# A fused attention and feed-forward kernel on one core: its 2074 steps emitted in another order

## The chip, the core and the metric

The kernel runs on one core of a Trainium2 chip. A core has five engines with a queue of instructions each: TensorE (PE, matmuls, with its weight loads shown as PEld), VectorE (DVE), ScalarE (ACT), GpSimd (POOL) and SyncE (SP). Here SP issues all transfers. Each queue is worked through in the order in which the program emitted its instructions; between queues only semaphores order the work. The metric is device time in microseconds, the median of repeated runs.

## The reference

Inputs q, k and v are (8, 8, 576, 64): batch, head, token, head width. Two attentions are added and the sum goes through a feed-forward block:

```python
# pooled: means over 4 tokens, softmax attention over 144, repeated 4 times
out_up = repeat(softmax(scale * q_d @ k_d.T) @ v_d, 4)
# local: a band of |i - j| < 4
out_local = softmax(where(abs(i - j) < 4, scale * q @ k.T, -1e9)) @ v
x = (out_up + out_local)            # as (4608 tokens, 512)
h = x @ w_in                        # 512 -> 1024
solu = h * softmax(h)
ln = (solu - mean) / sqrt(var + 1e-6) * g_ln
out = ln @ w_out                    # 1024 -> 512
```

The weights come as 64-bit floats. The products of the feed-forward block are done in three parts (high x high, high x low, low x high) to keep their precision.

## The kernel before, in words

The work is cut into steps, and a step is what a Python generator does between two `yield`s: mostly one engine's instructions. A list `plan` holds all 2074 of them in a fixed numbering (lines 948 to 959), and `ORDER` (lines 26 to 125) is a list of these numbers. Lines 961 to 964 turn the scheduler off and call the steps in `ORDER`'s sequence, so that `ORDER` is the program order, and its projection on each engine is that engine's queue. Buffers rotate in this sequence too: a tile with a tag of one buffer can be taken only when the last reader of the tile before is done.

The steps, by the names that the text uses:

- **Batch b, prepare** (`load_q_k`, then `pair_steps` for each of four pairs of heads): q and k are loaded and transposed, in batches 0 to 2 on TensorE (`qp`, `kp`, line 463, with ScalarE's copy at 469), from batch 3 on VectorE (lines 390 and 394). VectorE then sums groups of four tokens (`qds`, `kds`, line 348). The q and k tiles have tags of one buffer.
- **Batch b, values**: four loads `vs` (line 260) with GpSimd sums (lines 415 and 418).
- **Batch b, local, five blocks u** (`by_tensor`): load `lv` (line 249); `sc` 32 small matmuls (591); on VectorE mask and maximum (603, 608); on GpSimd a subtraction (610); on ScalarE exp (612); on VectorE sum and reciprocal (615, 619); on GpSimd a product (621); on TensorE `plt`, four transposes (631); ScalarE's copy (634); `xp`, 32 matmuls (641); and the result goes into x (480 on ScalarE, 482 on VectorE).
- **Batch b, pooled, four pairs** (`Pooled`): `sd` (667), maximum (674), exp (682 to 686), reciprocal (689), GpSimd's product (691), `pdt` (702), two copies (709 on ScalarE, 714 on VectorE from batch 2 on), `po` (723), and VectorE's addition into x (482; in batch 0 it is ScalarE's copy that begins x).
- **Weights, 16 pieces** (`Weights`): a load (297), ScalarE's absolute value (305), four VectorE steps (307, 311, 316, 320) that make a 32-bit float out of the halves of a 64-bit one, a rounding to the high part on ScalarE (341; pieces 8 to 15 are multiplied by g_ln first, 339), and the low part on GpSimd (343). Pieces 0 to 7 are w_in, 8 to 15 w_out.
- **Tile i of 128 tokens, in** (`xhl`, `ffn_in`): ScalarE's cast xh (890), GpSimd's rest xl (893), `h` in two halves of 12 large matmuls (741), maximum on VectorE (749), exp on ScalarE (753), product on VectorE (756), small GpSimd steps (761, 765), ScalarE's shift by the mean (778), the write of the tile to DRAM as `u` (784), a reciprocal (787), the sum of squares (793) and the small steps to the scale s (790 to 800). `ffn_back` reads `u` back as `v`, rearranged, in four transfers (816).
- **Tile i, out** (`ffn_ut`, `ffn_out`): two VectorE transposes of 32x32 blocks (837), ScalarE's cast uh (843) and the rest ul (845, GpSimd; VectorE from tile 29 on) for each half, `o` in two halves of 12 large matmuls (859), ScalarE's scaling to osb (866), and the store (868). Tile 35 is transposed by TensorE instead (`ut`, 833).

PSUM has eight banks and is divided thus: `ps_a` two tiles of two banks (`sc`, `sd`, `pdt`, `xp`, `qp`, `kp` in turn), `ps_t` one bank (`plt` and `po`; in batches 0 and 1 every other one goes to `ps_o`), `ps_h` two banks (`h`), `ps_o` one bank (`o`).

In the old list the part from batch 2 on is regular: one `h` and one `o` of 24 large matmuls in turn, with one to four small blocks between them.

Of the kernel before, what the change touches and what calls it, by code (L numbers as in the profile page):

```python
# [128 lines left out]
def pooled_local_attention_then_solu_ffn(  # L129
# [142 lines left out]


    class Weights:
        def begin(self):
            stage = att.tile([P, NPR, S], F32, tag="x", name="stage", bufs=2)
            self.stage = stage.rearrange("p a s -> p (a s)")
            self.g = cpool.tile([P, NFC], F32, name="g_sb")
# [718 lines left out]
```

## Time and profile before

| | |
|---|---|
| median of 3 runs | 630.46 us (628.94 to 631.41) |
| span of the profiled execution | 627.6 us (its own time isn't given beside it) |
| TensorE busy | 577.7 us, 92% |
| VectorE, ScalarE, GpSimd busy | 393.4, 370.4, 380.8 us |
| chain that ended last | TensorE 62%, VectorE 11%, SP's queue 8%, transfers 7% |
| bytes moved by the transfers | 94.31 MB, 150 GB/s on average |

The span runs from the first to the last instruction of one execution. Lines of the profile name the source line, engine, operation, output and inputs, shapes, and a count; busy time is followed by the mean in ns; "[0.61 <-DVE x L482]" is idle time ahead of an instruction and what ended it. In the rows of busy time by stretches the columns are the stretch, its length, then busy us (and instructions) of PE, PEld, DVE, ACT and POOL, the granted clock of TensorE (1.00 is full), the busy share of the DMA engines, and GB/s.

### The profile page before, as it was taken

The numbers are of one execution on the slowest core, as the hardware profiler recorded it, in microseconds if no ns is written. First come the engines' busy times: TensorE is split into PE (matmuls) and PEld (weight loads), VectorE is DVE, ScalarE is ACT, GpSimd is POOL, SyncE is SP. The second block draws the span as 40 slices with busy tenths as digits, with TensorE's granted clock in tenths as the row PEclk, the third lists the DMA queues.
The fourth block names the chain that finished last, engine by engine and source line by source line (L and its number), as shares of the span: only waits on it lengthen the run. The fifth ranks groups of instructions, "written<-read, shape, count | busy, mean of one in ns | idle before, by whom it ended". The sixth has DMA issues, their size and how long they took to land.

```text
span 627.6 us, 14806 instructions
## 1 busy us (share of the span) xinstructions
PE 577.7 (92%) x5624; PEld 451.6 (72%) x5624; DVE 393.4 (63%) x684; ACT 370.4 (59%) x808; POOL 380.8 (61%) x552
## 2 busy tenths in 40 slices
PE   1677789989999998999999899999999999999997
PEld 1456557777777776777777677777777777788875
DVE  6988869775745683678536783679356534453541
ACT  3667586865753565547745575556855675454451
POOL 2486668969734894469636893589646974242210
PEclk9985879969999998999999899999999999999999
DMA  9997994668668878664678477824542232224320
GB/s 233 263 195 210 191 218 119 175 131 174 157 173 177 179 177 180 165 170 139 158 160 196 120 172 154 192 95 138 159 142 71 70 118 85 85 84 154 98 101 34
DMA packets 210055, 94.31 MB, mean 150 GB/s; under 512 B 171712, under 2 KB 198848, under 8 KB 209984
## 3 DMA queue, kind: packets, MB, share of 16 engines
q1 hardware_dynamic: 209984, 93.37, 60.1%
q8 instruction: 44, 0.72, 0.5%
q14 instruction: 27, 0.22, 0.1%
HBM read 65.54 MB, written 27.79 MB: 149 GB/s over the span
## 4 chain that ended last, share of the span: by engine, by line
PE 62%; DVE 11%; SPq 8%; DMA 7%; ACT 5%; issue 4%; POOL 3%; DVEq 0%; POOLq 0%; ACTq 0%
PE o L859 25%; PE h L741 23%; SPq L230 4%; DMA v<-u 3%; PE xp L641 3%; PE plt L631 3%; PE po L723 2%; DMA u<-e 2%; PE sd L667 2%; SPq L816 2%; PE sc L591 2%; DVE w L316 1%; DVE nmx L749 1%; DVE v L837 1%; PE pdt L702 1%
## 5 line engine op out<-in xcount | busy, mean ns | idle before, releaser
L859 PE MATMUL o<-wo_h,uh 128*128 128x512 f32 x288 | 118.8, 412 | 4.3 <-ACT uh L843 3.6
L741 PE MATMUL h<-wi_h,xh 128*128 128x512 f32 x288 | 119.9, 416 | 3.0 <-ACT xh L890 2.7
L741 PE MATMUL h<-wi_h,xl 128*128 128x512 f32 x288 | 116.7, 405 | 0.5 <-POOL xl L893 0.4
L741 PE MATMUL h<-wi_l,xh 128*128 128x512 f32 x288 | 116.3, 404 | 0.0
L859 PE MATMUL o<-wo_l,uh 128*128 128x512 f32 x288 | 115.6, 401 | 0.0
L845 POOL TENSOR_TENSOR ul<-v,uh 128x512 fp32r<-128x512 f32 x58 | 74.5, 1293 | 25.3 <-ACT uh L843 20.4
L749 DVE TENSOR_REDUCE nmx<-h 128x1 f32<-128x1024 f32 x36 | 43.6, 1212 | 59.8 <-PE h L741 59.8
L859 PE MATMUL o<-wo_h,ul 128*128 128x512 f32 x288 | 79.4, 397 | 0.2 <-POOL ul L845 0.2
L859 PEld LDWEIGHTS o<-wo_h,uh 128*128 128x128 f32 x288 | 55.1, 191 | 18.5 <-ACT uh L843 4.0
L741 PEld LDWEIGHTS h<-wi_h,xh 128*128 128x128 f32 x288 | 55.7, 193 | 16.7 <-ACT xh L890 3.1
L741 PEld LDWEIGHTS h<-wi_h,xl 128*128 128x128 f32 x288 | 55.4, 192 | 15.4 <-POOL xl L893 2.0
L859 PEld LDWEIGHTS o<-wo_h,ul 128*128 128x128 f32 x288 | 54.6, 190 | 14.1 <-POOL ul L845 0.7
L741 PEld LDWEIGHTS h<-wi_l,xh 128*128 128x128 f32 x288 | 55.9, 194 | 12.1
L837 DVE STREAM_TRANSPOSE v<-v 128x512 f32<-128x512 f32 x70 | 46.6, 691 | 27.9 <-DMA v<-u 27.6
L859 PEld LDWEIGHTS o<-wo_l,uh 128*128 128x128 f32 x288 | 55.2, 192 | 12.0
L843 ACT ACTIVATE uh<-v 128x512 fp32r<-128x512 f32 x70 | 43.5, 625 | 27.6 <-DVE v L837 18.9
L753 ACT ACTIVATE e<-h,nmx 128x1024 f32<-128x1024 f32 x36 | 40.1, 1113 | 32.4 <-DVE nmx L749 32.0
L893 POOL TENSOR_TENSOR xl<-x,xh 128x512 fp32r<-128x512 f32 (+1 forms) x40 | 47.3, 1185 | 19.4 <-ACT xh L890 19.3
L610 POOL TENSOR_TENSOR pl<-pl,mxl 128x512 f32<-128x512 f32 x40 | 42.4, 1068 | 22.6 <-DVE mxl L608 22.5
L793 ACT ACTIVATE e<-e 128x1024 f32<-128x1024 f32 x35 | 36.9, 1054 | 31.3 <-DMA u<-e 31.0
L778 ACT ACTIVATE e<-e,nmu 128x1024 f32<-128x1024 f32 x35 | 40.2, 1147 | 18.1 <-POOL nmu L761 18.0
L621 POOL TENSOR_TENSOR pl<-pl,rsl 128x512 f32<-128x512 f32 x40 | 42.0, 1056 | 13.8 <-DVE rsl L619 10.0
(92 smaller groups left out, 1084.9 us busy)
## 6 DMA issues: line engine op xcount, KB each, us to landing
u<-e SPq DMA_DIRECT2D x35, 512.0 KB
v<-u SPq DMA_DIRECT2D x140, 128.0 KB
vw<-in_v_dram SPq DMA_DIRECT2D x160, 64.0 KB
vs<-in_v_dram SPq DMA_DIRECT2D x32, 288.0 KB
out_dram<-osb SPq DMA_DIRECT2D x36, 256.0 KB
qm<-in_q_dram SPq DMA_DIRECT2D x80, 72.0 KB
km<-in_k_dram SPq DMA_DIRECT2D x80, 72.0 KB
w<-in_moe_w_out_dram SPq DMA_DIRECT2D x8, 512.0 KB
```

The source lines that it names most:

```text
L610: nc.gpsimd.tensor_tensor(out=pl, in0=pl, in1=max_bc, op=ALU.subtract)
L621: nc.gpsimd.tensor_tensor(out=pl, in0=pl, in1=rs.unsqueeze(3).broadcast_to([P, NPR, 2, W]), op=ALU.mult)
L741: nc.tensor.matmul(hps[:, n, :], src[:, cc, :], wt[:, cc, n * 512:(n + 1) * 512], start=(cc == 0 and src is xh and wt is wi_h), stop=(cc = ...
L749: nc.vector.tensor_reduce(out=nmx, in_=hf, op=ALU.max, axis=AX.X, negate=True)
L753: nc.scalar.activation(e, hf, AF.Exp, bias=nmx, scale=1.0, accum_out=se)
L778: nc.scalar.activation(e, e, AF.Identity, bias=nmu, scale=1.0)
L793: nc.scalar.activation(e0, e, AF.Square, accum_out=m2)
L837: nc.vector.transpose(vg, vg)
L843: nc.scalar.activation(uh, tp, AF.Copy)
L845: (nc.vector if v is None or i in LATE else nc.gpsimd).tensor_tensor(out=ul, in0=tp, in1=uh.bitcast(F32), op=ALU.subtract)
L859: nc.tensor.matmul(o, src[:, j, :], wt[:, 4 * g + j, :], start=(g == 0 and j == 0 and src is uh and wt is wo_h), stop=(g == 1 and j == 3 a ...
L893: nc.gpsimd.tensor_tensor(out=l, in0=src, in1=h.bitcast(F32), op=ALU.subtract)
```

## The change

The list `ORDER` is another permutation of the same steps. Three things in the code go with it, so that steps of a batch can come in any sequence: a batch's buffers are made when first asked for (`__getattr__`) and no longer by the step of pair 0; the weights' staging buffer is made by the first piece that uses it; and the load of g_ln is a step of its own, number 2074. No operation, size, engine or buffer count changes.

```diff
 ORDER = """
-136 144 152 0 160 137 168 138 7 139 145 140 146 141 147 142 148 143 176 149 153 184 150 1 154
-155 192 151 2 3 156 14 161 157 4 5 158 6 159 36 162 169 163 21 170 8 37 171 38 164 172 9 10 39
...
-2035 2036 2037 2020 2000 2021 2054 2038 2040 2039 2022 2055 2056 2041 2023 2057 2042 2043 2058
-2059 2060 2044 2061 2024 2062 2025 2047 2045 2063 2046 2048 2064 2049 2065 2066 2050 2067 2068
-2069 2070 2071 2072 2073
+136 137 138 139 144 145 140 141 142 146 143 147 148 152 153 149 150 151 154 155 156 157 0 1 160
+7 2 3 4 5 161 162 6 8 9 163 164 165 166 10 11 168 12 13 36 14 167 158 46 37 47 159 169 170 192
...
+2019 2020 2035 2036 2014 2037 2021 2053 2054 2022 2055 2023 2056 2057 2038 2058 1975 2059 2064
+2040 2041 2039 2042 2043 2044 2024 2025 2060 2061 2045 2047 2046 2048 2065 2066 2049 2050 2067
+2068 2062 2069 2063 2070 2071 2072 2073
 """
...
     class Weights:
-        def begin(self):
-            stage = att.tile([P, NPR, S], F32, tag="x", name="stage", bufs=2)
-            self.stage = stage.rearrange("p a s -> p (a s)")
-            self.g = cpool.tile([P, NFC], F32, name="g_sb")
-            with nc.allow_non_contiguous_dma(reason="one small vector"):
-                nc.sync.dma_start(self.g, g_ln.rearrange("(fc p) -> p fc", p=P))
+        def __init__(self):
+            self.stage = None
...
+        def load_g(self):
+            self.g = cpool.tile([P, NFC], F32, name="g_sb")
+            with nc.allow_non_contiguous_dma(reason="one small vector"):
+                nc.sync.dma_start(self.g, g_ln.rearrange("(fc p) -> p fc", p=P))
...
+        def __getattr__(self, what):
+            if what == "qk":
+                self.qk = self.room()
+            elif what in ("qT", "kT"):
+                setattr(self, what, att.tile([P, NPR, S], F32, tag=what, name=f"{what}_{self.b}"))
...
+    step(weights.load_g)
```

Numbers 0 to 27 are batch 0's prepare, 28 to 35 its values, 36 to 75 pooled, 76 to 135 local, 136 to 263 the weights (eight a piece), 264 to 363 tiles 0 to 3; batch 1 begins at 364, batch 2 at 625, batch 3 at 861, batch 4 at 1114, and so on to tile 35, which begins at 2051.

Read by engine, the two lists differ thus. **SP at the start**, `wl` a weight piece, `qk` a pair of q and k, `vs` and `lv` values:

```
before: g wl0 wl1 wl2 qk0.0 wl3 wl4 qk0.1 wl5 wl6 wl7 qk0.2 qk0.3 vs0.0 vs0.1 wl8 vs0.2 lv0.0 qk1.0
after:  wl0 wl1 wl2 qk0.0 wl3 qk0.1 wl4 qk0.2 wl7 qk0.3 wl5 vs0.0 vs0.1 wl9 qk1.0 qk1.1 vs0.3 qk1.2
```

**TensorE**, batch 4 to 5 (a number after the dot is the block or pair), where the small blocks stand closer together in the new list:

```
before: o13 pdt4.1 po4.1 sc5.0 pdt4.2 h16 po4.2 sc5.1 pdt4.3 o14 po4.3 sc5.2 sc5.3 plt5.0 h17
after:  o13 xp4.4 pdt4.1 po4.0 pdt4.2 sc5.2 po4.1 h16 pdt4.3 po4.2 sc5.3 sc5.1 po4.3 sc5.4 sd5.0 plt5.0 o14
```

**The end** of TensorE's queue (o a, o b are halves):

```
before: h35 o33 o34a o34b ut35a ut35b o35
after:  h35 o33 ut35a o34a o34b ut35b o35
```

**SP's queue at tile 18**: the new list has, between the tile's write (784) and its read back (816), the values `lv6.0`, the read back of tile 17 and the store of tile 15. The old list has one load of q and k there.

More of the change, by code (lines that the diff above doesn't have):

```diff
@@ L285, in begin @@
             self.raw = {}
+        def load_g(self):
+            self.g = cpool.tile([P, NFC], F32, name="g_sb")
+            with nc.allow_non_contiguous_dma(reason="one small vector"):
+                nc.sync.dma_start(self.g, g_ln.rearrange("(fc p) -> p fc", p=P))
         def load(self, n):
-            if n == 0:
-                self.begin()
             if n in (0, 1, 6, 7):
+                if self.stage is None:
+                    stage = att.tile([P, NPR, S], F32, tag="x", name="stage", bufs=2)
+                    self.stage = stage.rearrange("p a s -> p (a s)")
                 hl = self.stage[:, n % 2 * 1024:n % 2 * 1024 + 1024]
@@ L357, in __init__ @@
             self.vw, self.vs = {}, {}
+        def __getattr__(self, what):
[3 more added lines that the diff above has]
+                setattr(self, what, att.tile([P, NPR, S], F32, tag=what, name=f"{what}_{self.b}"))
+            elif what == "qd":
+                self.qd = [
+                    qd_flat[:, (NPR - 1 - pr) * SD:(NPR - pr) * SD] for pr in range(NPR)
+                ]
+            elif what == "kd":
+                self.kd = att.tile([P, NPR, SD], F32, tag="kd", name=f"kd_{self.b}", bufs=2)
+            elif what == "vd":
+                self.vd = att.tile([72, 2, H, D], F32, tag="vd", name=f"vd_{self.b}")
+            else:
+                raise AttributeError(what)
+            return self.__dict__[what]
         def room(self):
-            b = self.b
-            self.qk = {
-                nm: load.tile([P, NPR, NB, 32], F32, tag=f"{nm}m", name=f"{nm}m_{b}")
+            return {
+                nm: load.tile([P, NPR, NB, 32], F32, tag=f"{nm}m", name=f"{nm}m_{self.b}")
                 for nm in ("q", "k")
@@ L366, in load_q_k @@
         def load_q_k(self, pr):
-            if pr == 0:
-                self.room()
             load_q_k(self.qk, self.b, pr)
@@ L372, in load_v @@
             self.vw[u] = load_vw(self.b, u)
-        def begin(self):
-            b = self.b
-            self.qT = att.tile([P, NPR, S], F32, tag="qT", name=f"qT_{b}")
-            self.kT = att.tile([P, NPR, S], F32, tag="kT", name=f"kT_{b}")
-            self.qd = [
-                qd_flat[:, (NPR - 1 - pr) * SD:(NPR - pr) * SD] for pr in range(NPR)
-            ]
-            self.kd = att.tile([P, NPR, SD], F32, tag="kd", name=f"kd_{b}", bufs=2)
         def pair_steps(self, pr):
-            if pr == 0:
-                self.begin()
             kT = self.kT[:, pr]
@@ L412, in pooled_vsum @@
             vs = self.vs.pop((c, hs.start))
-            if (c, hs.start) == (0, 0):
-                self.vd = att.tile([72, 2, H, D], F32, tag="vd", name=f"vd_{self.b}")
             nc.gpsimd.tensor_tensor(
@@ L429, in room @@
         def room(self):
-            self.qk = {}
+            qk = {}
             n = self.TT * 2 * D
@@ L434, in room @@
                 for pr in range(3):
-                    self.qk[nm, pr] = t[:, pr * n:(pr + 1) * n]
+                    qk[nm, pr] = t[:, pr * n:(pr + 1) * n]
+            return qk
         def load_q_k(self, pr):
-            if pr == 0:
-                self.room()
             for nm, src in (("q", q), ("k", k)):
@@ L451, in pair_steps @@
         def pair_steps(self, pr):
-            if pr == 0:
-                self.begin()
             HT = self.TT // 2
```

186 rows, old and new, of the table ORDER are left out of this document.

## The prediction

> **What bounds the kernel now.** I read the page first, then busy time by stretches, the waits of TensorE, its timeline, the chain, and the groups by shape.
>
> ```profile
> span 627.6 us, 14806 instructions
> PE 577.7 (92%) x5624; PEld 451.6 (72%) x5624; DVE 393.4 (63%) x684; ACT 370.4 (59%) x808; POOL 380.8 (61%) x552
> ```
>
> TensorE is busy for 577.7 of 627.6 us, and its matmuls stay the same, so only its 49.9 us of idle time, and what it loses at a halved clock, can go. Busy time by stretches, and VectorE's first step on the weights in its timeline, say where those are:
>
> ```profile
> 0.00:64.00 64.00, 36.15 (x457) 29.39 (x458) 52.38 (x88) 39.77 (x97) 36.80 (x40) 0.82 0.97 226
> 242.60:246.00 3.40, 0.53 (x4) 0.46 (x3) 1.93 (x3) 1.18 (x3) 0.47 (x1) 1.00 0.99 288
> 246.00:249.40 3.40, 3.40 (x9) 2.61 (x9) 0.94 (x2) 3.40 (x8) 3.40 (x4) 0.50 0.77 127
> 345.00:348.40 3.40, 1.05 (x18) 0.90 (x11) 3.04 (x6) 2.17 (x5) 1.66 (x3) 1.00 0.22 87
> 348.40:351.80 3.40, 3.40 (x9) 2.63 (x9) 1.34 (x3) 1.59 (x4) 3.32 (x4) 0.50 0.62 194
> ```
>
> ```profile
> 6.82 0.43 DVE L307 TENSOR_SCALAR w<-w 128x512 f32<-128x512 f32 x1 [3.68 <-ACT w L305]
> ```
>
> In the first 64 us TensorE idles for 27.85 us (64.00 less 36.15), more than half of all its idle time. VectorE is busy for 52.38 of those 64, and has nothing but small fills before its first weight piece at 6.82 us, which leaves it about 5 us of slack: up to there VectorE is the bound. The other four rows show the second loss: a stretch in which TensorE stands still is followed by 3.4 us at clock 0.50, which costs another 1.7 us.
>
> The later stalls are these, from TensorE's timeline:
>
> ```profile
> 205.40 0.63 PE L631 MATMUL plt<-ident,pl 128*128 128x128 f32 x4 [0.61 <-DVE x L482]
> 245.50 0.50 PE L859 MATMUL o<-wo_h,uh 128*128 128x512 f32 x1 [2.88 <-ACT uh L843]
> 277.63 0.63 PE L631 MATMUL plt<-ident,pl 128*128 128x128 f32 x4 [0.34 <-DVE x L482]
> 347.51 0.63 PE L631 MATMUL plt<-ident,pl 128*128 128x128 f32 x4 [2.35 <-DVE x L482]
> 416.46 0.63 PE L631 MATMUL plt<-ident,pl 128*128 128x128 f32 x4 [0.69 <-DVE x L482]
> 610.33 0.50 PE L859 MATMUL o<-wo_h,uh 128*128 128x512 f32 x1 [0.78 <-ACT osb L866]
> 617.78 0.50 PE L859 MATMUL o<-wo_h,uh 128*128 128x512 f32 x1 [0.69 <-ACT uh L843]
> ```
>
> Four wait for VectorE to add a `po` block to x (L482), which frees the one-bank tile that the first `plt` of the next batch takes. But three of the seven come from a transfer, as the chain shows:
>
> ```profile
> 240.06 3.82 DMA v<-u
> 244.07 0.72 DVE v L837
> 340.08 5.25 DMA v<-u
> 345.36 0.71 DVE v L837
> 411.19 3.06 DMA v<-u
> 414.37 1.31 DVE v L837 x2
> 564.57 5.62 PE h L741 x24
> ```
>
> VectorE had come to a tile's transposes (L837) before the tile was back from DRAM, and everything queued behind them stood still: the stalls that end at 245.50, 347.51 and 416.46 follow within 2.1 us of these transposes.
>
> **The change, part by part.** No instruction is added or taken away; only the order within each queue changes, and with it which step stands ahead of which. `g` goes from the head of SP's queue to place 22, and only the scaling of the w_out pieces (L339) needs it, which stands later still: nothing. Tiles made at first use cost nothing by themselves. The rest I read by counting, for a step of TensorE, what each queue must have done before it.
>
> *Start to tile 1.* The last early place where VectorE binds is tile 1's first product:
>
> ```profile
> 78.89 0.80 PE L741 MATMUL h<-wi_h,xh 128*128 128x512 f32 x1 [1.44 <-ACT xh L890]
> 85.78 0.66 PE L667 MATMUL sd<-kd,qd_flat 64*64 64x144 f32 x12
> 86.37 0.50 PE L741 MATMUL h<-wi_h,xh 128*128 128x512 f32 x1
> 89.38 0.92 PE L702 MATMUL pdt<-ident,pd 64*72 64x64 f32 x24
> ```
>
> ```profile
> L749 DVE TENSOR_REDUCE nmx<-h 128x1 f32<-128x1024 f32 x36 | 43.6, 1212 | 59.8 <-PE h L741 59.8
> L756 DVE SCALAR_TENSOR_TENSOR e<-h,e 128x1024 f32<-128x1024 f32 x36 | 43.6, 1211 | 9.6 <-ACT e L753 9.4
> L603 DVE TENSOR_TENSOR pl<-sc,mask 128x512 f32<-128x512 f32 x40 | 26.6, 680 | 8.7 <-PE sc L591 8.4
> L482 DVE TENSOR_TENSOR x<-x,po 128x576 f32<-128x576 f32 x28 | 20.8, 742 | 16.3 <-PE po L723 16.2
> L316 DVE SCALAR_TENSOR_TENSOR w<-w,w 128x512 int32<-128x512 int32 x12 | 10.9, 927 | 0.0
> L307 DVE TENSOR_SCALAR w<-w 128x512 f32<-128x512 f32 x16 | 10.3, 661 | 5.5 <-ACT w L305 5.5
> L311 DVE TENSOR_SCALAR w<-w 128x512 int32<-128x512 int32 x16 | 9.4, 610 | 0.1
> L320 DVE SCALAR_TENSOR_TENSOR w<-w,w 128x512 int32<-128x512 int32 x12 | 8.9, 768 | 0.0
> ```
>
> VectorE no longer has in front of it tile 0's L749 and L756 (1.21 + 1.21) nor piece 11's four steps (0.66 + 0.61 + 0.93 + 0.77 = 2.97); one reduction is swapped for another of its kind, and a small reciprocal that comes in I leave out. That is 5.4 us less. Meanwhile TensorE gets one `sd` and one `pdt` block more done: 0.59 us (85.78 to 86.37) and half of 0.92, together 1.0. So -6.4, if VectorE binds there and nothing else is late next. What is late next are ScalarE's cast xh and GpSimd, and both also have less in front of them in the new lists; the transfers ahead of that product fall from 14.3 to 13.7 MB. The deferred steps come back by tile 8, where VectorE is no longer the bound (393.4 busy in 627.6). Ends: 0 and, if short forms come in as well, the third rival.
>
> *Round trips through DRAM.* In the old list there are 8 tiles for which less than 11 us of TensorE work lie between the end of their `h` (L741) and the steps that VectorE must wait out before it comes to their transposes. Tile 20, for instance, has the two halves of `o` 18, 5.6 us like the 24 matmuls in the last row of the chain, and six small blocks. In the new list there are 3 (tiles 0, 18 and 28). The transfer-made stalls (2.88 + 2.35 + 0.69 = 5.9) and the two halved stretches behind them (2 x 1.7) make 9.3 us; three eighths, 3.5, stay: -5.8. Ends: -9.3 and 0. Tile 18 is the weakest place, with 1.05 MB between its write and its read back in SP's queue.
>
> The row first: 2.88 us idle at 245.50 and 2.35 at 347.51 were each followed by 3.4 us at half clock. The Trainium skill, TensorE: Matmul & The Clock Gate, HAM oscillation, gives as the abstract rule that only idle gaps over some 3.4 us matter. By it these two gaps would cost only themselves, and the sum would gain 2.1 us less (five eighths of 3.4). The trace disagrees, and decides.
>
> *The one-bank tile.* `plt` and `po` share it from batch 2 on. In 53 successions the old list has 5 with under 1.3 us of TensorE work in between, always the last `po` of a batch and the next `plt`; the new list has 14, among them six from `po` to `po`. Of the five, two were transfer-made (347.51, 416.46), one didn't wait and two cost 0.61 and 0.34: 0.32 each over three. 14 x 0.32 = 4.5, less 0.95 now: +3.5. Ends: -0.95, and 14 x 2.35 - 0.95 = +32.
>
> *The pairs of banks.* `sc`, `sd`, `pdt` and `xp` take two tiles in turn. From batch 3 on the old list never has under 6 us of TensorE work between a block and the next user of its tile; the new list has under 1.3 us at 23 of 88 places, where small blocks are bunched. The nearest row is the one run of bunched blocks now, behind tile 3's last product, from 121.54 to the end of the last row:
>
> ```profile
> 121.54 0.69 PE L641 MATMUL xp<-plT,vw 64*64 64x58 f32 x32
> ...
> 127.03 0.69 PE L641 MATMUL xp<-plT,vw 64*64 64x56 f32 x32 [0.51 <-ACT plT L634]
> 129.07 0.46 PE L591 MATMUL sc<-kT,qT 64*64 64x64 f32 x15 [1.10 <-issue]
> ```
>
> 1.61 us in 12 blocks, 0.13 each: 23 x 0.13 = +3.1. Ends: 0 and 23 x 0.51 = +11.7.
>
> *The end.* `ut` is split round `o` 34, so the wait for osb at 610.33 and the one for uh at 617.78 have TensorE work in front of them: -0.78 - 0.69 = -1.5. Ends: -1.5 and 0. The drain after the last product stays.
>
> Sum: -6.4 - 5.8 + 3.5 + 3.1 - 1.5 = -7.1, a span of 620.5 us. The profiled execution's own time is known only as its span, 627.6; the median of the runs, 630.46, is 2.9 above it. With the same 2.9: 623.4 us.
>
> **The rivals.**
>
> *The one-bank tile decides (slower).* Bunching makes VectorE late at most of the 14 places. At the last `po` of batch 4 the new queue holds, ahead of its L482, another L482 and two L603 whose blocks come immediately before: 0.74 + 0.68 + 0.68, then its own 0.74, against 1.17 us of TensorE work (`sc` and `sd`) before the next `plt`: 1.67 us late. At 14 places that is 23.4 - 0.95 = 22.4 instead of 3.5: +11.8 in all, 639.4 + 2.9 = 642.3 us. It is slower by 0.5% (3.2 us) from 1.05 us a place on. For it: 2.35 has happened. Against it: at most of the 14 places VectorE's steps ahead were released 5 us earlier.
>
> *The early gain is eaten (no change).* `o` 0, ahead of tile 3's `h` on TensorE in both lists, has 84.0 us of VectorE work in front of it instead of 80.8, by the same durations. If that place binds, the -6.4 goes: 626.9 + 2.9 = 629.8 us. Against it: `o` 0 started without a wait.
>
> *VectorE's steps shrink too (much faster).*
>
> ```profile
> 7.74 0.69 DVE L316 SCALAR_TENSOR_TENSOR w<-stage,w 128x512 int32<-128x512 int32 x1
> 13.22 1.63 DVE L316 SCALAR_TENSOR_TENSOR w<-w,w 128x512 int32<-128x512 int32 x1
> ```
>
> ```profile
> 12.86 1.44 POOL L343 TENSOR_TENSOR wi_l<-w,wi_h 128x512 fp32r<-128x512 f32 x1 [1.30 <-ACT wi_h L341]
> ```
>
> L316 takes 0.69 alone and 1.63 beside a GpSimd product that ends at 14.30. Of L307, 16 x (0.66 - 0.43, the first row at 6.82) = 3.7, and of L316, 12 x (0.93 - 0.69) = 2.8, are such waiting; in the new order GpSimd has 39 us in front of tile 1 instead of 45, so less may collide. All of the 6.5 gone: 616.9 us. The Trainium skill, SBUF — State Buffer, two separate sides, calls the pair of ports that the two engines share an exclusive lock, whose loser is fully blocked; this trace agrees, with the 1.63. The collisions may as well grow, which is in the range's upper part.
>
> **How the numbers follow.** Forecast 623.4 us (618 to 627), chance 0.43; shrinking steps, below 618, 0.19; no change 0.18; one-bank tile, 0.20. A measurement here tells about 0.5% from no change, 627.3 to 633.6. Faster 0.62, same 0.18, slower 0.20. The range leaves out a tenth at each side: below, rival three together with all round trips mended (616.9 - 3.5) and two thirds of the 6.6 us for bunching gone, 609; above, nearly to the one-bank rival's price, 640.
>
> **What would show it.** Right: tile 1's `h` starts at about 73 us; no half-clock stretch behind a VectorE wait for v<-u after 150 us; `plt` and `po` waiting for L482 in many short pieces, 4 to 5 us in all; nothing idle ahead of the last two `o`. Wrong: tile 1 still at 78 or later; or the waits for L482 and for evacuations adding up to over 15 us; or tile 18's transposes holding VectorE long enough to bring a new half-clock stretch.

## The result, and the profile after

The kernel with the new order takes 610.97 us (median of 4 runs, 608.56 to 611.85) against 629.70 before (628.81 to 631.41): a ratio of 0.9704, 95% interval 0.9671 to 0.9738. The forecast was 623.4. The page's first lines for the kernel after; its profiled execution took 611.77 us around a span of 610.0:

```profile
span 610.0 us, 14785 instructions
PE 570.7 (94%) x5624; PEld 449.4 (74%) x5624; DVE 393.6 (65%) x684; ACT 366.0 (60%) x808; POOL 376.8 (62%) x552
```

Busy time by stretches (columns as before), first two rows of the kernel before that were not shown, then the kernel after:

```profile
64.00:115.00 51.00, 43.88 (x507) 33.16 (x507) 41.85 (x73) 36.64 (x81) 39.16 (x45) 0.89 0.78 164
115.00:146.00 31.00, 29.39 (x463) 23.64 (x463) 21.53 (x38) 18.88 (x36) 23.95 (x31) 0.83 0.70 171
```

```profile
0.00:64.00 64.00, 39.76 (x475) 31.76 (x476) 53.92 (x91) 39.93 (x102) 35.66 (x41) 0.93 1.00 225
64.00:115.00 51.00, 45.81 (x523) 36.57 (x522) 42.67 (x73) 38.64 (x79) 34.04 (x39) 0.92 0.72 168
115.00:146.00 31.00, 30.88 (x499) 24.49 (x498) 22.68 (x38) 19.81 (x45) 26.33 (x36) 1.00 0.75 174
215.40:218.80 3.40, 3.02 (x7) 2.44 (x8) 3.40 (x5) 2.95 (x6) 2.90 (x7) 0.50 0.75 134
250.00:350.00 100.00, 99.92 (x1010) 78.49 (x1006) 69.98 (x128) 60.29 (x138) 70.71 (x105) 1.00 0.69 164
350.00:450.00 100.00, 99.83 (x1063) 78.76 (x1067) 65.17 (x119) 62.33 (x142) 71.48 (x106) 1.00 0.62 154
```

The column to read is PE's, with the clock behind POOL's: from 115 to 146 us TensorE now works almost without a break (30.88 of 31.00 us) at full clock, where it idled 1.6 us and had clock 0.83, and from 250 to 450 us it idles 0.25 us in all. Of the 17.6 us of span, 10.6 are idle time of TensorE (49.9 us before, 39.3 now) and 7.0 are busy time of the same 5624 matmuls (577.7 and 570.7), fewer of which ran at half clock: the clock of the first three stretches is 0.82, 0.89 and 0.83 before and 0.93, 0.92 and 1.00 after. TensorE's stalls of over 0.3 us behind 70 us, from its timeline:

```profile
75.94 0.86 PE L701 MATMUL pdt<-ident,pd 64*72 64x64 f32 x12 [3.48 <-DVE x L481]
114.75 0.63 PE L630 MATMUL plt<-ident,pl 128*128 128x128 f32 x4 [0.32 <-ACT osb L865]
215.78 0.79 PE L858 MATMUL o<-wo_h,uh 128*128 128x512 f32 x1 [2.92 <-ACT uh L842]
241.49 0.50 PE L740 MATMUL h<-wi_h,xl 128*128 128x512 f32 x1 [0.91 <-POOL xl L892]
592.61 0.50 PE L858 MATMUL o<-wo_h,uh 128*128 128x512 f32 x1 [0.38 <-ACT osb L865]
600.19 0.50 PE L858 MATMUL o<-wo_h,uh 128*128 128x512 f32 x1 [1.26 <-ACT osb L865]
```

(Most lines have moved up by one: L858 is `o`, L740 `h`, L481 the addition into x.)

To place a gain I use a ledger: the time at which a tile's `h` starts, less the TensorE work issued before it, every block at its duration at full clock (12 large matmuls 2.81 us, a small block 0.5 to 0.66). What is left is time lost so far. It holds for different orders, since work done sooner is credited. In us, worked out from the traces:

```
at             tile 1  tile 4  tile 8  tile 11  tile 18  tile 22  last o
before          48.1    61.4    62.8    68.3     74.8     76.4     80.1
after           46.0    49.0    50.3    55.4     57.7     58.9     62.5
```

The 17.6 us by which the spans differ came 2.1 before tile 1, 10.3 between tiles 1 and 4, 0.5 from there to tile 11, 4.2 from 11 to 18, and 0.5 behind that.

### The profile page after: what moved, and what is told of

The parts are those of the page before. It is cut to its first block, busy times and chain, and to the rows that moved or that the text cites. A ratio compares the mean times of both kernels' runs of the same rounds, so it can differ in the third digit from the quotient of the medians.

```text
span 610.0 us, 14785 instructions
## 1 busy us (share of the span) xinstructions
PE 570.7 (94%) x5624; PEld 449.4 (74%) x5624; DVE 393.6 (65%) x684; ACT 366.0 (60%) x808; POOL 376.8 (62%) x552
## 4 chain that ended last, share of the span: by engine, by line
PE 59%; DMA 9%; DVE 8%; POOL 7%; SPq 7%; issue 5%; ACT 4%; POOLq 0%; DVEq 0%; ACTq 0%
PE o L858 24%; PE h L740 22%; DMA v<-u 3%; PE xp L640 3%; SPq L230 2%; DMA qm<-in_q_dram 2%; PE plt L630 2%; PE po L722 2%; DMA km<-in_k_dram 2%; PE sd L666 2%; PE sc L590 2%; DMA u<-e 2%; DVE w L318 2%; POOL pl L609 1%; POOL ul L844 1%
## 5 line engine op out<-in xcount | busy, mean ns | idle before, releaser
L858 PE MATMUL o<-wo_h,uh 128*128 128x512 f32 x288 | 117.7, 409 | 4.7 <-ACT uh L842 2.9
L740 PE MATMUL h<-wi_h,xh 128*128 128x512 f32 x288 | 118.4, 411 | 0.2
L740 PE MATMUL h<-wi_h,xl 128*128 128x512 f32 x288 | 115.5, 401 | 0.9 <-POOL xl L892 0.9
L740 PE MATMUL h<-wi_l,xh 128*128 128x512 f32 x288 | 115.5, 401 | 0.0
L858 PE MATMUL o<-wo_l,uh 128*128 128x512 f32 x288 | 114.8, 399 | 0.0
L858 PE MATMUL o<-wo_h,ul 128*128 128x512 f32 x288 | 79.0, 396 | 0.0
L858 PEld LDWEIGHTS o<-wo_h,uh 128*128 128x128 f32 x288 | 54.8, 190 | 18.9 <-ACT uh L842 3.7
L836 DVE STREAM_TRANSPOSE v<-v 128x512 f32<-128x512 f32 x70 | 46.9, 691 | 33.6 <-DMA v<-u 29.5
L740 PEld LDWEIGHTS h<-wi_h,xh 128*128 128x128 f32 x288 | 55.3, 192 | 14.9 <-issue 0.8
L740 PEld LDWEIGHTS h<-wi_h,xl 128*128 128x128 f32 x288 | 55.1, 191 | 15.0 <-POOL xl L892 1.6
L740 PEld LDWEIGHTS h<-wi_l,xh 128*128 128x128 f32 x288 | 55.3, 192 | 12.2
L858 PEld LDWEIGHTS o<-wo_h,ul 128*128 128x128 f32 x288 | 54.2, 188 | 13.4 <-POOL ul L844 0.2
L858 PEld LDWEIGHTS o<-wo_l,uh 128*128 128x128 f32 x288 | 54.8, 190 | 12.1
L755 DVE SCALAR_TENSOR_TENSOR e<-h,e 128x1024 f32<-128x1024 f32 x36 | 43.8, 1216 | 21.4 <-ACT e L752 21.2
L620 POOL TENSOR_TENSOR pl<-pl,rsl 128x512 f32<-128x512 f32 x40 | 41.7, 1046 | 13.2 <-DVE rsl L618 5.1
L417 POOL TENSOR_TENSOR vs<-vs 72x512 f32<-72x512 f32 x32 | 41.4, 1295 | 9.1 <-DMA vs<-in_v_dram 8.9
```

Source lines behind the costliest of these rows:

```text
L417: nc.gpsimd.tensor_tensor(out=vs[:, :, 0:2 * D], in0=vs[:, :, 0:2 * D], in1=vs[:, :, 2 * D:4 * D], op=ALU.add)
L620: nc.gpsimd.tensor_tensor(out=pl, in0=pl, in1=rs.unsqueeze(3).broadcast_to([P, NPR, 2, W]), op=ALU.mult)
L740: nc.tensor.matmul(hps[:, n, :], src[:, cc, :], wt[:, cc, n * 512:(n + 1) * 512], start=(cc == 0 and src is xh and wt is wi_h), stop=(cc = ...
L755: nc.vector.scalar_tensor_tensor(out=e, in0=hf, scalar=1.0, in1=e, op0=ALU.mult, op1=ALU.mult, accum_out=su)
L836: nc.vector.transpose(vg, vg)
L858: nc.tensor.matmul(o, src[:, j, :], wt[:, 4 * g + j, :], start=(g == 0 and j == 0 and src is uh and wt is wo_h), stop=(g == 1 and j == 3 a ...
```

## The experiments

Each kernel was timed in turn with the kernel before; ratios are to that, with 95% intervals. "Old" and "new" are the two orders. All share the new kernel's code, and only queue orders differ.

### Is it the order, and do its stretches add up?

The first theory was that gains are local: whatever the new order wins by tile 4 stays won if the old order follows. The rival: it is lent, by side work put off.

```diff
 a0_before_list:  ORDER = the old list (g first)
 a1_after_to_t4:  ORDER = new list up to "h of tile 4", then the rest in the old sequence
 a2_before_to_t4: ORDER = old list up to "h of tile 4", then the rest in the new sequence
 c1_after_to_t8:  as a1, the seam at "h of tile 8"
```

> The new code (buffers made at first use, g_ln's load a step of its own, put first) with the list of before. Theory (the order alone makes the gain): 630 us, within 0.5% of before. Rival (where the buffers come to lie changes something): 3 us or more away from before.

> The new list up to the step that begins tile 4's first product, then what is left in the old list's sequence. Time less the TensorE work done, read at tile 4, is 12.3 us lower in the new kernel than in the old. Theory (the gains are local and add up: 12.3 up to tile 4, 4.9 between tiles 16 and 18, the rest nothing): 630 - 12 = 618 us. Rival 1 (it is given back later, where the old list has its waits on transfers): 624 or more. Rival 2 (the early part does it all): 612.

> The other half: the old list up to tile 4's first product, then the new list. Theory (local gains that add up): 630 - 5 = 625 us. Rival 1 (the later part of the new list gains only with what the early part leaves ready): 630. Rival 2 (the bunched blocks of the later part cost where the queues are less far ahead): 632 or more.

> The new order up to tile 8's h product, the old order from there. At tile 8 both orders have issued almost the same steps (VectorE 227 and 227, TensorE 139 and 139), so the early part has put nothing off that the late part needs at once. Theory (gains of a stretch add up when nothing is put off at the seam): 50.3 us lost at tile 8, as in the new order, and then the old order's 17.3 us: about 615 to 618 us. Rival (the new order's early gain is always given back behind the seam, as it was with the seam at tile 4): 626 to 632 us.

Measured: a0 627.87 us, 0.9969 (0.9928 to 1.0011); a1 631.46, 1.0031 (0.9996 to 1.0066); a2 624.28, 0.9902 (0.9868 to 0.9937); c1 629.03, 1.0031 (0.9995 to 1.0067). The code alone changes nothing that these runs can tell. The early part by itself brings nothing either, and the late part about 1%, which is not the whole. a2 came out at the 625 us that the local theory gave, but a1 and c1 are 13 and 11 us above what it gave for them. The ledger shows how the early gain goes:

```
at             tile 1  tile 4  tile 8  tile 11  tile 18  tile 22  last o
a1 (new to 4)   46.1    61.4    64.5    73.6     76.4     83.1     86.7
c1 (new to 8)   47.1    50.0    57.6    69.8     73.1     75.6     79.2
a2 (old to 4)   45.5    63.4    68.2    69.6     71.9     72.8     77.1
```

c1 keeps 11.4 us up to tile 4 and is back at the old order's loss at tile 11. So the theory falls, in a1 and in c1: with the seam at tile 8, where both orders have issued almost the same steps, the gain was still gone. Part of it goes right at the seam, and that is put-off work: GpSimd's `pl` product (L620) stood behind work that ScalarE released late, and TensorE waited 5.95 us for it:

```profile
200.38 1.12 PE L630 MATMUL plt<-ident,pl 128*128 128x128 f32 x4 [5.95 <-POOL pl L620]
```

The other 12.2 us go between tiles 8 and 11.

### SyncE's queue

SyncE issues all 628 DMAs of the kernel, at 0.50 us each (median in the traces), in order. From 180 to 270 us it spends 82.7 of 90 us issuing in the old order, 82.2 in c1, and 70.5 in the new order. Its timeline in c1, start and duration ahead of the line, from which TensorE's small blocks have their loads and the tiles their read-backs:

```profile
184.14 2.19 SPq L230 DMA_DIRECT2D qm<-in_q_dram  x4
186.37 2.12 SPq L230 DMA_DIRECT2D km<-in_k_dram  x4
188.54 2.12 SPq L230 DMA_DIRECT2D qm<-in_q_dram  x4
190.70 3.37 SPq L230 DMA_DIRECT2D km<-in_k_dram  x4
194.17 2.58 SPq L249 DMA_DIRECT2D vw<-in_v_dram  x4
```

Each row ends where the next begins. So a read-back comes when the DMAs ahead of it are through, whatever TensorE has won: DMAs ahead of it, and when it was issued (us):

```
read-back of   tile 6        tile 8        tile 10
old            247 (203.8)   295 (238.6)   335 (265.1)
c1             208 (176.2)   295 (239.9)   335 (265.8)
new            208 (175.8)   268 (216.9)   295 (243.8)
```

c1 was 16.5 us ahead of the old order at tile 7 (173.1 against 189.6 us), and its read-backs of tiles 8 and 10 went out 1.3 and 0.7 us later than the old order's. The Trainium skill, Perfetto Trace Analysis, section What "DMA-bound" means, names this case: a kernel can be bound by the issuing sequencer when its track is solid DMA slices. The trace agrees, for this stretch. Five kernels test it by moving SyncE's loads, and some stores with them, and nothing on the other queues:

```diff
 f1: c1,  loads that new has behind the read-backs of tiles 7..19 moved behind them
 f5: f1,  the same up to tile 26
 f2: old, the same from tile 2 on
 f6: old, tiles 7..26, only loads with 20 us of TensorE work before their reader
 f3: new, loads that old has ahead of the read-backs of tiles 2..19 moved ahead
```

> The run with the new order up to tile 8 and the old one behind it, with SyncE's loads for later batches put behind the read-backs of tiles 7 to 19 wherever the new order has them behind. No other queue is touched. Read-back of tile 8 then stands behind 265 DMAs on SyncE in place of 295, that of tile 10 behind 293 in place of 335, at 0.50 us each. Theory (the old order's late part is held by SyncE, which issues without a break from 180 to 270 us, so that an early gain runs into it and is lost): the loss between tile 7 and tile 11 (50.4 to 69.8 us) is cut to under 10 us and the kernel takes 612 to 620 us. Rival (the round trips are late for another reason, or the loads are now late): 625 to 632 us, as without the change.

> The old order with the same done to it from tile 2 on, SyncE's queue alone. Read-back of tile 3 behind 147 DMAs in place of 171, of tile 6 behind 208 in place of 247, of tile 10 behind 293 in place of 335. Theory (SyncE's queue holds the old order from tile 3 on): the round trips come sooner, the loss at tiles 10 and 16 to 18 (9 us in all) and part of that at tiles 3 and 4 goes: 616 to 624 us. Rival (in the old order TensorE's early loss leaves SyncE time enough, and the loads are wanted when they stand there): 627 to 633 us.

> The converse: the new order, with loads put ahead of the read-backs of tiles 2 to 19 wherever the old order has them ahead. SyncE's queue alone. Read-back of tile 6 behind 243 DMAs in place of 208, of tile 10 behind 331 in place of 295. Theory: SyncE issues without a break to about 270 us again, TensorE waits for read-backs, and 5 to 15 us of the gain go: 616 to 626 us. Rival (the loads' place in the queue doesn't matter): within 3 us of the new order.

> The run with the new order up to tile 8 and SyncE's loads put off behind it, done to tile 26 in place of tile 19. In that run 51 DMAs were left between the read-backs of tiles 19 and 20, SyncE issued them until 423 us, tile 20's transposes waited, and TensorE stood for 20.19 us at 429.75 and ran at half clock around it. Here at most 43 stand between two read-backs (45 in the new order). Theory (SyncE's queue): that wait goes, the loss is 60 to 62 us at tile 11 as before and under 72 at the end: 612 to 620 us. Rival (the wait comes back at another tile): over 625 us.

> The old order, SyncE's queue alone: loads put behind the read-backs of tiles 7 to 26 where the new order has them behind, and only if 20 us of TensorE's work lie between the load and its first reader. Read-back of tile 8 behind 269 DMAs in place of 295, of tile 10 behind 293 in place of 335, of tile 18 behind 450 in place of 491. Theory (what the old order loses at tiles 10 and 16 to 18, 9 us, is SyncE's queue): 619 to 625 us. Rival (the old order's late losses have another cause, or the loads come too late): 627 us or more.

Measured: f1 646.91 us, 1.0258 (1.0203 to 1.0314); f2 663.27, 1.0528 (1.0476 to 1.0579); f3 783.99, 1.2461 (1.2397 to 1.2525); f5 634.05, 1.0153 (1.0084 to 1.0223); f6 644.02, 1.0290 (1.0219 to 1.0361). Every time that the theory gave was missed; only the open-ended rivals of f5 (over 625 us) and f6 (627 or more) hold. The ledger says in which stretch:

```
at             tile 4  tile 8  tile 11  tile 18  tile 22  last o
c1              50.0    57.6    69.8     73.1     75.6     79.2
f1              48.5    55.9    60.7     68.4     92.3     96.0
f5              48.9    56.0    58.2     65.2     79.7     83.3
old             61.4    62.8    68.3     74.8     76.4     80.1
f6              57.1    59.5    59.8     71.3     87.7     91.3
```

Between tiles 8 and 11 the theory holds: 12.2 us lost in c1, 4.8 in f1, 2.2 in f5; 5.5 in the old order, 0.3 in f6. The wait of 2.88 us at 245.50 in the old order, with the slow stretch behind it, was SyncE's queue: it is absent in f6, and there with 2.1 to 5.6 us in the other runs with that queue (a1, b1, b2, c1, c2, e1). f2, which isn't in the table, goes the other way: it lost some 11 us from tile 4 to tile 8 and as much from there to tile 11, because the moved loads were now late themselves. VectorE waited 11.55 us for a load of k, up to 154.08 us, TensorE 6.37 us for what stood behind it, and later five times for `lv`, 2.9 us in all. Behind tile 20 the same edits do harm, by a mechanism of the same kind: TensorE stood for 20.19 us in f1, 19.93 in f2, 10.93 in f5 and 12.70 in f6. In f5 34 DMAs stand between the read-back of tile 19 and the write of tile 20; ScalarE's square of tile 20 works in place and must wait for that write, and what is queued behind it makes TensorE wait. ScalarE's row, then TensorE's, of f5:

```profile
411.17 1.06 ACT L792 ACTIVATE e<-e 128x1024 f32<-128x1024 f32 x1 [11.39 <-DMA u<-e]
```

```profile
417.82 1.09 PE L630 MATMUL plt<-ident,pl 128*128 128x128 f32 x4 [10.93 <-DVE x L481]
```

In the new order 8 DMAs stand between those two. f3 shows the size of what is at stake: VectorE waited 203.8 us for read-backs (29.5 in the new order), though SyncE issued for only 36.6 of 90 us from 180 to 270; it was held by loads whose buffers were not yet free (61.4 us for line 249 alone), with read-backs behind them. So a queue full of DMAs is one way of being late there, and a load that waits for its buffer another.

### Squares that wait for their write

In the old order ScalarE waits 31.0 us, 16 times, for a tile's write to DRAM before it may square the tile; in the new order 1.1 us, once. That looked like a cause.

```diff
 e1: old, on ScalarE: "square of tile i" moved behind later steps (4.3 -> 7.2 us behind its input on average)
 e2: new, on ScalarE: "square of tile i" moved ahead                (10.1 -> 7.3 us)
```

> The old order, with the step that squares a tile's result in place (it may not start before the tile's write to DRAM has landed) moved back on ScalarE: 7.2 us of ScalarE's own work between the step that makes the result and the square on average, in place of 4.3 us (10.1 us in the new order). Nothing else moves. Theory (ScalarE's queue, stopped 31.0 us in all by squares that wait for their write in the old order and 1.1 us in the new, is what makes the old order late): the waits fall below 12 us, and the kernel ends 5 to 12 us sooner, 617 to 624 us. Rival (ScalarE has the time to spare, and TensorE's stalls come from elsewhere): the waits fall as far, and the time stays within 2 us of the old order's.

> The converse: the new order, with the squares moved forward on ScalarE, 7.3 us of its work behind the step that makes the result on average in place of 10.1 us (and 4.5 us where the other queues allow it). Theory: squares wait for their writes again, 6 to 15 us in all, and the kernel ends 3 to 8 us later than the new order, 614 to 619 us. Rival: the waits come back and the time stays within 2 us of the new order's.

Measured: e1 662.95 us, 1.0551 (1.0494 to 1.0607); e2 617.87, 0.9836 (0.9788 to 0.9883). The waits are down to 2.6 us in e1, as the first row shows, and it is 33 us slower:

```profile
ACT e L792 <- DMA u<-e: 2.6, 3, 1.5
```

```profile
DVE v L836 <- DMA v<-u: 53.6, 20, 7.0
```

VectorE now waits 53.6 us for read-backs in place of 27.6. e2 lost 7 us though its squares waited only 1.8 us. Both theory and rival fall: the time doesn't follow those waits. Whether they cost the old order anything is not shown, because the later square brought waits of its own: e1 loses some 25 us behind tile 22, where the old order loses under 4.

### Round trips: transposes behind an addition

```diff
 c2: old, on VectorE
-... vtr(15) r(16) vtr(15) add(po 4.3) ...   ... vtr(20) vtr(20) add(po 5.3) ...
+... r(16) add(po 4.3) vtr(15) vtr(15) ...   ... add(po 5.3) vtr(20) vtr(20) ...
```

> The old order, with one addition on VectorE at each of two places (batch 4's pooled product 3, batch 5's) put ahead of the transposes of tile 15 and of tile 20, which wait there for their data from DRAM. Theory (the term of the prediction for the round trips: the transposes hold up the addition behind them, and with it the bank that TensorE needs): the waits of 2.35 us at 347.51 and 0.69 us at 416.46 go, and with them the half clock from 348.4 to 351.8 (1.7 us): 4 to 5 us sooner, 624.5 to 626 us. Rival (TensorE then waits for the transposes' own products, or for the next step): under 1.5 us.

Measured: 626.56 us, 0.9961 (0.9933 to 0.9989). The waits at 347.51 and 416.46 are gone; the loss from tile 16 to 18 is 1.6 us in place of 4.2, but 1.6 came back as a wait for plT at 433.26. The prediction's mechanism is there, at about half the size expected. The ledger alone would not show it: b1, whose queues are the old order's there, lost no more between these tiles, since its wait was 0.92 us and no half clock followed; but both waits are in b1 and b2 (0.92 and 2.04, 2.15 and 1.68 us) and neither is in c2.

### Bunched small blocks

```diff
 d3: new, at ten places where the next plt or po follows at once
-VectorE: ... add(po 4.2) pl+(5.3) pl+(5.1) ...
+VectorE: ... pl+(5.3) pl+(5.1) add(po 4.2) ...
```

> The new order with the step that frees the single bank of the small products put behind the next two steps of its engine's queue, at ten of the places where the next small product follows with under 1.3 us of TensorE work between (nine additions on VectorE, one eviction on ScalarE). Theory (bunching cost nothing because the engine that frees the bank stands idle for exactly that step): TensorE now waits 0.7 to 1.7 us at each, 8 to 15 us in all, 619 to 626 us. Rival (the bank was never what TensorE waits for there): under 3 us more.

Measured: 631.10 us, 1.0060 (1.0021 to 1.0099), some 20 us slower than the new order. TensorE's waits for these steps, none of which is in the new order's list (total, times, longest):

```profile
PE plt L630 <- DVE x L481: 5.4, 3, 2.1
PE po L722 <- DVE x L481: 4.5, 3, 1.7
PE plt L630 <- ACT plT L633: 3.6, 1, 3.6
```

The theory holds, and is dearer than its 8 to 15 us, since four stretches of 3.4 us at half clock come with the waits. In the new order the step that frees the bank is the next in its engine's queue, and the engine stands waiting for it: VectorE sat idle 14.5 us, ten times, until a `po` was done.

### Tile 1, tile 7 and the end

In the new order tile 1's `h` came at 77.94 us, not at 73. VectorE's timeline says why:

```profile
69.23 1.05 DVE L309 TENSOR_SCALAR w<-w 128x512 f32<-128x512 f32 x1
70.32 0.43 DVE L313 TENSOR_SCALAR w<-w 128x512 int32<-128x512 int32 x1
70.78 1.66 DVE L318 SCALAR_TENSOR_TENSOR w<-w,w 128x512 int32<-128x512 int32 x1
72.48 1.63 DVE L322 SCALAR_TENSOR_TENSOR w<-w,w 128x512 int32<-128x512 int32 x1
74.03 1.21 DVE L748 TENSOR_REDUCE nmx<-h 128x1 f32<-128x1024 f32 x1
75.17 0.62 DVE L481 TENSOR_TENSOR x<-x,xp 128x464 f32<-128x464 f32 x1
75.71 0.60 DVE L673 TENSOR_REDUCE mxd<-sd 128x3 f32<-128x432 f32 x1
76.65 1.22 DVE L755 SCALAR_TENSOR_TENSOR e<-h,e 128x1024 f32<-128x1024 f32 x1 [0.34 <-ACT e L752]
```

Piece 11's four steps and tile 0's two reductions are all done before tile 1's `h`, which starts at 77.94, 0.07 us after the last of them ends.

```diff
 d1: new, on VectorE
-... w4(11) w5(11) nmx(0) add(xp 0.3) mxd(1.1) hE(0) ...
+... nmx(0) add(xp 0.3) mxd(1.1) hE(0) w4(11) w5(11) ...      (w4, w5: L318, L322)
 d2: d1 + ScalarE: uh(7) ahead of exp(3.1); the end: vtr1(35) ahead of o(34), osb(34) ahead of uh(35)
 d4: d1 + ScalarE: plT(0.4) qT(1.3) kT(1.3) ahead of the steps of piece 13
```

> The new order with three of VectorE's steps (the row maximum of tile 0, the addition that frees the bank TensorE waits 3.48 us for, the exponent product of tile 0) moved ahead of the last two steps of weight piece 11, and the steps that follow from it on ScalarE and GpSimd. Theory (tile 1 came at 78 and not at 73 because a bank that TensorE's own queue needs was freed late): tile 1's h starts at 74.5 to 75.5 us, the half-clock stretch at 75.4 to 82.3 shortens or goes, and the kernel ends 3 to 6 us sooner, 605 to 608 us. Rival (what is won there is waited for again before tile 4): within 1 us of the new order.

> As the run before it, and two more places: ScalarE copies tile 7's transpose ahead of the exponentials of batch 3's pooled product 1 (the second half of the transpose ahead of one VectorE step for it), and at the end tile 35's second transpose and tile 34's eviction are put ahead of their neighbours. Theory: the wait of 2.92 us at 215.78 shrinks to under 1 us and the 3.4 us at half clock behind it (1.7 us) go; the wait of 1.26 us ahead of the last o product goes: 4 to 5.5 us less than the run before it, 600 to 604 us. Rival (other queues are as tight there): under 1 us less.

> The run with tile 0's steps ahead of piece 11 on VectorE, and besides, on ScalarE, the evictions of the first bank pair of batch 1's last projection (and one plT) ahead of the steps of piece 13 that waited for VectorE there; in that run TensorE waited 2.57 us for this at 84.83 and lost what tile 1 had won. Theory (what tile 1 wins is kept if the next queue is cleared too): tile 2's h 2 to 4 us sooner than there, 86 us, tile 4's at 126 to 129 us, the kernel at 604 to 607 us. Rival (the next queue behind it takes it back): within 1 us of that run, 608 to 610 us.

Measured: d1 608.97 us, 0.9713 (0.9639 to 0.9788); d2 608.90, 0.9704 (0.9645 to 0.9763); d4 609.86, 0.9676 (0.9641 to 0.9711). None differs measurably from the new order's 0.9704. TensorE's timeline of d1, then of d4:

```profile
75.04 0.50 PE L740 MATMUL h<-wi_h,xh 128*128 128x512 f32 x1 [0.75 <-DVE e L755]
84.83 1.12 PE L640 MATMUL xp<-plT,vw 64*64 64x56 f32 x32 [2.57 <-ACT qT L468]
```

```profile
74.94 0.50 PE L740 MATMUL h<-wi_h,xh 128*128 128x512 f32 x1 [0.76 <-DVE e L755]
84.13 0.53 PE L701 MATMUL pdt<-ident,pd 64*72 64x64 f32 x12 [1.20 <-ACT wo_h L343]
87.00 1.99 PE L590 MATMUL sc<-kT,qT 64*64 64x64 f32 x64 [2.34 <-DVE x L481]
```

Tile 1 comes 3 us sooner, as the theory had it, and TensorE waits for it ten microseconds later, in d1 for ScalarE, in d4 with that cleared for VectorE. Tile 4's `h` starts at 131.8 us in the new order and d1, at 132.3 in d4. The rival held both times: something else is late next. d2's two other edits brought nothing to see: the wait at 215.78 was already absent in d1, where nothing near it had changed (0.9 us lost from tile 8 to tile 10, 5.0 in the new order's profile), so it comes in some executions and not in others, and the end lost 1.6 us behind tile 35's `h` in place of 2.0.

### The dense stretch at 121 to 140 us

In the old order TensorE stops 0.51 and 1.10 us among the small blocks and then runs at half clock for 10.3 us. A row by stretches of the kernel before:

```profile
129.90:140.20 10.30, 10.30 (x98) 7.78 (x94) 8.63 (x16) 4.55 (x11) 6.64 (x8) 0.50 0.66 139
```

```diff
 b1: old, TensorE: o(1) ahead of the last small blocks, in place of behind them
 b2: old, SyncE:   vs(2.1) vs(2.2) vs(2.3) vs(3.0) eight steps (some 30 DMAs) later
```

> The old list with one move: tile 1's o (24 large matmuls, and its osb) go from behind 20 small blocks to the place ahead of local block 4's xp of batch 1, so that the run of small blocks from 121.5 us on is broken in two. In the old trace the clock drops to 0.50 at 129.9 us, after 1.6 us of waiting among small blocks, and stays there for 10.2 us, which costs 5.1. Theory (the halved stretch comes of the wait among small blocks and lasts until large matmuls come): no halved stretch near 130 us, 5 to 6 us less, 625. Rival (TensorE then waits for tile 1's ul or for osb, or the small blocks behind drop the clock all the same): 629 to 632, with a half-clock stretch within 15 us.

> The old order, with four loads of values (288 KB each, three of batch 2 and one of batch 3, not read before some 30 us later) issued some 10 DMAs later on SyncE, so that they don't run while TensorE works through the dense small blocks at 121 to 129 us. Theory (the stop of 1.10 us inside a block at 129.07, which no wait explains, comes from the DMA rings being full, and the half clock from 129.9 to 140.2 from that stop): both go, tile 4's h starts 5 to 6.5 us sooner, and the kernel ends 0 to 6 us sooner. Rival (the stop comes from the density of the small products alone): stop and half clock stay, tile 4 within 1 us.

Measured: b1 629.35 us, 1.0022 (0.9987 to 1.0058); b2 633.49, 1.0064 (1.0023 to 1.0105). In both the stop of 1.10 us is gone. But b1 has waits of 1.43 and 1.89 us soon after, a half clock from 141.4 to 148.3 us, as its rival had it, and the same loss at tile 4 (61.2); and b2, with no half clock near 130 us, is 2.7 us better at tile 4 and then loses 7.8 to tile 7, where the old order loses 0.5. That the stop came from the loads is not shown: c2, whose queues are the old order's up to here, had no such stop, and f6's, also unchanged here, was 0.20 us. What the old order loses up to tile 4 varies so, from execution to execution, from 57.1 (f6) to 63.4 (a2); the new order's runs have 48.5 to 50.0.

## Why the prediction was wrong, step by step

The direction was right; of the 17.6 us of span it had 7.1. The two steps that cost it most are the first two below.

- **Start to tile 1, -6.4: failed.** Measured -2.1 in the ledger, -1.0 in time. The failed step is "VectorE no longer has in front of it tile 0's L749 and L756 ... nor piece 11's four steps". Tile 1's `h` takes the same two banks as tile 0's, which are free only when these two have read them; I counted which steps `h` needs for its data and forgot its buffer. And `pdt` ahead of it on TensorE waited for a bank that VectorE freed behind piece 11. d1 and d4 add that even the 3 us that could be had there go to the next queue. Nor has the sum a term for the clock of this stretch, 0.82 in its first row and 0.93 after.
- **Tile 1 to tile 4, nothing: failed, the largest miss.** It was worth 10.3. The old order has seven waits there (0.39, 0.81, 0.96, 0.26, 1.15, 0.51, 1.10: 5.2 us) and 16.9 us at half clock, up to 85.6 us and from 129.9 to 140.2 (8.5 lost); the new one waits 0.24, 0.27 and 0.32 us and is at half clock for 4.3, up to 82.3 (2.2 lost). That makes 13.7 and 3.0, the ledger's difference within 0.4. No single row looked worth a term, and I didn't add them up. The half clock at 130 us is not the steady part: it is 10.2 us in the run before and in a2, 3.4 in c2, and absent in f6. The gain is: with the old queues up to there the runs lose 10 to 18 us in this stretch (f6, a2), with the new ones 2 to 4 (f5, d3). One wait is in all eight runs with TensorE's old queue there, 1.0 to 2.5 us at 90 to 95 us, in all but the run before with a half clock of 3.4 or 6.8 us beginning beside it: `qp` and `kp` follow two `pdt` blocks at once and wait for the copies that free their banks. In the new list the first of the two stands ahead of tile 1's `h`. It is a reading of the traces, and no run moved it alone. Which difference of the order brings the whole was not isolated; b1 and b2 each took the stop away and got other waits.
- **Round trips, -5.8: about right, for a cause partly missed.** The old order's stalls made by them and the slow stretches behind them were 9.3 us; one is left, 2.92 and 1.7, so -4.7. It is at tile 7, which the count of three tiles didn't have, not at 18, and absent in d1's execution. The first of the old ones (245.50) is SyncE's queue, which f6 showed and I had not looked at; the other two are transposes ahead of an addition, which c2 showed.
- **One-bank tile, +3.5, and pairs of banks, +3.1: mis-sized.** Both are 0: from 250 to 450 us TensorE idles 0.25 of 200 us, and the waits for banks behind tile 1, up to the end, add up to under 1 us. I priced 14 places by three of the old order where the freeing step had stood in a queue. d3 shows what it costs where it does stand so: seven waits, 13.5 us.
- **The end, -1.5: failed.** 0.38 and 1.26 us are left, in place of 0.78 and 0.69: on ScalarE osb of tile 34 stood behind uh of tile 35.
- **The rivals.** The one-bank rival is refuted. That the early gain is eaten is what happens in a1 and c1, when the old order follows, through SyncE's queue and work put off, and not at `o` 0 as it said. The measured time lies in the range of the third rival, but not by its mechanism: VectorE is busy for 393.6 us, as it was for 393.4, so its steps did not shrink.

Open: what in the new order makes the 10.3 us; which queue sets tile 4's time (d1 and d4 moved tile 1 and not tile 4); and why a2, with the new order from tile 4 on, loses 4.8 us up to tile 8 and yet gains 1% in all.

## What to carry to other kernels

Lay out, for the in-order queue that issues the DMAs, how many stand ahead of each transfer that someone will wait for, times the 0.5 us that each took: an early gain runs into that count, and a load put ahead too soon, or a pile of loads in one place, costs as much as a stall of the engines. Before a step is struck from what stands ahead of a product, ask for its buffer as well as its data. And an order found as a whole is fitted as a whole: halves of it, with the older one for the rest, gave 1% or nothing of its 3%, and a bunched block is free only as long as the step that frees its bank is next in its queue.

## What the runs showed of the hardware

- Stretches at half clock are multiples of 3.4 us long (3.4, 6.8, 10.2 and, in a1, 13.7), and small waits among small blocks are enough: in c2 waits of 0.55 and 0.31 us at 133 and 134 us were followed by this:

```profile
134.40:137.80 3.40, 3.40 (x11) 2.83 (x11) 3.33 (x8) 2.24 (x5) 3.32 (x5) 0.50 0.97 153
```

  The Trainium skill, TensorE: Matmul & The Clock Gate, section A second HAM failure mode: psum-queue depth-cycling, says that short idle times between groups of matmuls can make the clock go back and forth. The trace agrees. The new order's run of such blocks from 115 us, with a single wait of 0.32 us, stayed at clock 1.00.
- Size does not set how long SyncE takes to issue a DMA: 0.50 us for a load of 72 KB (median of 160) and 0.35 us for a tile's write of 512 KB (median of 35), though single ones took up to 2.7 us. It is the number of DMAs that counts.
- In the new order's execution VectorE's L318 took 0.69 us at 63.02, with GpSimd idle, and 1.66 at 70.78, with GpSimd in a product, as L316 had before.
